# Depthwise convolution and SwiGLU on one core: own input tiles for the first pair of each sequence, group 0's ScalarE products one chunk later, joins one chunk later, two swaps moved behind the marks

## The chip, the core and the metric

One NeuronCore of a Trainium2 chip runs the kernel. TensorE (PE) multiplies, VectorE (DVE), ScalarE (ACT) and GpSimd (POOL) work on tiles, SyncE (SP) issues most transfers. Each engine works through an instruction list of its own, in order. The metric is device time in microseconds of one execution; lower is better.

## What is computed

The reference, cut to what matters:

```python
# x: (8, 4096, 192) float32, weight: (8 heads, 7 taps)
w = softmax(weight, axis=-1)                       # 7 taps per head of 24 channels
x_pad = concatenate([zeros((B, 6, D)), x], axis=1) # each sequence starts from zeros
y[b, s, c] = sum_k w[head(c), k] * x_pad[b, s + k, c]
# y as (32768, 192); w_gate, w_val: (192, 1536); w_out: (1536, 192)
g = y @ w_gate
out = (g * sigmoid(g) * (y @ w_val)) @ w_out       # float32
```

A causal convolution with seven taps runs over each of the 8 sequences separately, and a gated feed-forward block over all 32768 tokens.

## The kernel before

**Tiling.** The tokens are cut into 64 blocks of 512, and two blocks make a pair `q` (1024 tokens, 32 pairs, four to a sequence: `ppb = 4`). The 1536 hidden columns are 12 chunks of 128 (`NCH`). A chunk of a block is the unit of the schedule: `first(j)` writes the gate and the value of chunk j with six matmuls (L397, L398; two at a time, one on each half of PE's rows), `gate(j)` takes silu on ACT (L402) and the product `h` on DVE (L404), and `second` does four output units (L409) that use the `h` of the block before. The gate has two PSUM buffers, so the gate matmuls of chunk j+2 wait for the silu of chunk j; the value has three.

**Convolution of the next pairs.** It runs beside these matmuls, on DVE, ACT and POOL, one to two pairs ahead. A pair has three groups: group 0 is channels 0 to 127 of its first block, group 2 the same channels of its second block, group 1 channels 128 to 191 of both blocks, on the two halves of the partitions. For each group, `plan_group` places these steps on chunks:

- `emit_load` (SP): four parts of x into the tiles `sqA` and `sqB`, as squares of 32 tokens by 32 channels, with 32 tokens of history (`HIST`) ahead.
- `emit_turn` (DVE, L100): transposes the squares into `xtA` or `xtB`.
- `emit_blank` (ACT, L104): only for `q % ppb == 0`, the first pair of a sequence: overwrites the history in `xtA` and `xtB` with zeros. There are seven such pairs (q = 4, 8, ..., 28); pair 0 has its own opening code.
- `start_d` (ACT, L334) and `dve_tap` (DVE, L344): a running sum of taps in `run`, at the end in `aD`.
- `act_tap` (ACT, L327): two products t; `pool_tap` (POOL, L349 and the add L356): two or three products, added up.
- `join` (POOL): adds ACT's two products (L356) and then `aD` (L362), which gives the convolved tile `xc`.
- `swap` (SP, L310 and L311): two transfers that copy `xc` into `xs` with its partition halves exchanged, which the matmuls need beside `xc`.

**Order.** `at_chunk(c, f)` hangs a step on chunk c. After a chunk's own instructions (matmuls, copy `o` L447 and store L439 where a half of a block is done, silu, product) the steps of that chunk follow in the order in which they were registered. A pair q is used from chunk 24q on. Its group 0 starts at 24q-28, group 1 at 24q-20, group 2 at 24q-12, and the offsets in `PLAN` count from there: the turn at -2, ACT's products at +2 and +4, DVE's taps at +1 and +3 (group 1 only +1), POOL's taps and the join at +4, the swap at +11. The second pair, `q == 2`, has its own swap offsets (`swap2`), pair 1 a table of its own (`opening`). The loads stand at 24q-47, -40, -34 and -28.

**Marks.** Two output units of opposite halves share a PSUM bank. Where the second half follows, PE must not begin before the first is done: `mark` (L304) puts an empty instruction into SP's list that waits for PE's last unit of the first half, and PE's next unit waits for this mark. Marks stand at chunks 1, 7, 13 and 19 of every 24, two at a time, ahead of the steps of the same chunk, and PE waits for them in the chunk that follows. SP's list holds marks, loads, swaps and stores in one order, so a swap that waits for its `xc` holds back every mark behind it.

**A pair in numbers of chunks, modulo 24.** Swaps before: group 0 at 7, group 1 at 15, group 2 at 23. ACT's copies `o`: at 4, 10, 16 and 22. ACT's steps for group 0: 20 (start), 22 and 0; group 1: 4, 6, 8; group 2: 12, 14, 16.

Of the kernel before, what the change touches and what calls it, by code (L numbers as in the profile page):

```python
# [11 lines left out]

PLAN = dict(
    start=(-28, -20, -12), turn=-2,
    acts=(2, 4), dves=(1, 3), pool=4, swap=11, swap2=(18, 16, 14), npool=(2, 3, 2),
    load=(-47, -40, -34, -28),
    opening=(
        (3, 5, (8,), (7, 9), 4, 10, 15),
        (9, 11, (12, 14), (13,), 11, 15, 21),
        (14, 16, (18, 20), (17, 18), 20, 20, 28),  # L20
    ),
# [5 lines left out]
def kernel(  # L27
# [9 lines left out]
    nc = tc.nc  # L37
    fp32 = mybir.dt.float32
# [5 lines left out]
    B, S, D = x.shape  # L44
# [3 lines left out]
    P = 128  # L48
    DB = D - P
    grp = D // H  # L50
    SUBS = 4
    TB = P * SUBS
    NCH = Dff // P
# [4 lines left out]
    n_pairs = NT // (2 * TB)  # L58
    ppb = S // (2 * TB)
    x_flat = x.flatten_outer_dims()  # L60

    const_pool = ctx.enter_context(tc.tile_pool(name="const", bufs=1))
    wpool = ctx.enter_context(tc.tile_pool(name="wts", bufs=1))
    xpool = ctx.enter_context(tc.tile_pool(name="xin", bufs=2))
# [8 lines left out]
    SQ = 32  # L73
    HIST = SQ
    squares, xts = {}, {}

    def emit_load(q, part):
        if part == 0:
            squares[q, "A"] = xpool.tile([P, HIST + 2 * TB], fp32, tag="sqA", name="sqA")
            squares[q, "B"] = xpool.tile([P, HIST + TB], fp32, tag="sqB", name="sqB")  # L80
        for k in range(2):
            quad = 2 * (part % 2) + k
            if part < 2:
                tile_, t0, n, c = squares[q, "A"], 0, 2 * TB, SQ * quad
            else:
                tile_, t0, n, c = squares[q, "B"], TB * (part % 2), TB, P + SQ * k
            row = q * 2 * TB + t0 - HIST
            n = n // SQ + 1
            nc.sync.dma_start(  # L89
                out=tile_[quad * SQ : (quad + 1) * SQ, :].rearrange("p (n c) -> p n c", c=SQ),  # L90
                in_=x_flat[row : row + n * SQ, c : c + SQ].rearrange("(n p) c -> p n c", p=SQ),
            )

    def emit_turn(q, g):
        name, lo, hi = (("A", 0, HIST + TB), ("B", 0, HIST + TB), ("A", HIST + TB, HIST + 2 * TB))[g]
        if g < 2:
            xts[q, name] = xpool.tile(
                list(squares[q, name].shape), fp32, tag=f"xt{name}", name=f"xt{name}"
            )
        nc.vector.transpose(out=xts[q, name][:, lo:hi], in_=squares[q, name][:, lo:hi])  # L100

    def emit_blank(q, g):
        rows = slice(0, (P, DB)[g])
        nc.scalar.copy(xts[q, "AB"[g]][rows, 0:HIST], zeros[rows, 0:HIST])  # L104

    def sync_after(ins, earlier, why="one bank, two halves of the array"):
        tc.add_manual_dep(
# [8 lines left out]
    for lo, hi in ((0, 2), (2, SUBS), (SUBS, 2 * SUBS)):  # L116
        nc.sync.dma_start(  # L117
            out=x_sb[:, lo:hi, :],
            in_=x_flat[lo * P : hi * P, :].rearrange("(s p) d -> p s d", p=P),
        )  # L120
    if n_pairs > 1:
        for part in range(4):
            emit_load(1, part)
# [10 lines left out]
    def load_w(lo, hi, which):  # L134
# [3 lines left out]
    zeros = const_pool.tile([P, TB], fp16, tag="zeros", name="zeros")  # L138
# [10 lines left out]
        out=mask, in_=mask, pattern=[[1, D]],  # L149
# [3 lines left out]
        out=mask, in_=mask, pattern=[[-1, D]],  # L153
# [315 lines left out]
    for k in range(1, 5):  # L469
        v, s = tapA1(k)  # L470
        nc.vector.scalar_tensor_tensor(
            out=sumA1, in0=v, scalar=s, in1=sumA1, op0=ALU.mult, op1=ALU.add
# [18 lines left out]
    def at_chunk(c, f):  # L491
        todo.setdefault(c, []).append(f)

    def plan_group(q, g, turn, start, acts, dves, pool, join, swap):
        made = []
        at_chunk(turn, lambda: emit_turn(q, g))
        if g < 2 and q % ppb == 0:
            at_chunk(start, lambda: emit_blank(q, g))

        def step(c, f):  # L500
            def run():
                if not made:
                    made.append(Group(q, g))
                f(made[0])

            at_chunk(c, run)

        ks = iter(range(1, K))
        step(start, lambda group: group.start_d())
        for k, c in zip(ks, acts):  # L510
            step(c, lambda group, k=k: group.act_tap(k))
        ks = list(range(1 + len(acts), K))
        for k, c in zip(ks, dves):
            step(c, lambda group, k=k: group.dve_tap(k, k == len(acts) + len(dves)))
        for k in ks[len(dves) :]:
            step(pool, lambda group, k=k: group.pool_tap(k))
        step(join, lambda group: group.join())
        step(swap, lambda group: group.swap())


    def lateC(step):
# [8 lines left out]
        else:  # L530
            nc.scalar.copy(D2b, late["sum"][:, 0, :])

    late = {}
    for step, c in enumerate((0, 1, 3, 5)):
        at_chunk(c, lambda step=step: lateC(step))

    if n_pairs > 1:
        for g, plan in enumerate(PLAN["opening"]):
            plan_group(1, g, *plan)
    for q in range(2, n_pairs):  # L540
        base = 2 * NCH * q
        for part, c in enumerate(PLAN["load"]):
            at_chunk(base + c, lambda q=q, part=part: emit_load(q, part))
        for g in range(3):
            c = base + PLAN["start"][g]
            plan_group(
                q, g, c + PLAN["turn"], c, [c + o for o in PLAN["acts"]],
                [c + o for o in PLAN["dves"][: 4 - PLAN["npool"][g]]],
                c + PLAN["pool"], c + PLAN["pool"],
                c + (PLAN["swap2"][g] if q == 2 else PLAN["swap"]),  # L550
            )


# [85 lines left out]
```

## Time and profile before

| | |
|---|---|
| median of 3 runs | 777.34 us (777.27 to 777.89) |
| profiled execution | 777.53 us, its span 775.8 us |
| PE busy | 768.8 us, 99% of the span |
| POOL busy | 669.2 us, 86% |
| DVE, ACT busy | 659.5 us, 659.4 us, 85% each |
| TensorE clock granted | 1.00 |
| 16 DMA engines, mean | 87 GB/s |

Busy time of PE is modelled and matmuls overlap, so 99% doesn't say that PE loses nothing: whether it does is seen from the starts of matmuls that should follow each other at a fixed distance. Times in the views are microseconds from the start of the span, and a line of the timeline gives start, duration, engine, line, operation and tiles, with the idle time ahead of it in brackets.

### The profile page before, as it was taken

What the parts mean: (1) busy time and instruction counts of PE and PEld (TensorE: products, weight loads), DVE (VectorE), ACT (ScalarE), POOL (GpSimd) and SP (SyncE); (2) the same over time, 40 slices, a digit from 0 to 9 for tenths busy, and PEclk for the clock granted to TensorE, in tenths of its full rate; (3) what the DMA queues carried; (4) which work ended last, traced back from release to release, by engine and by line L of the source; (5) the groups of instructions that cost most, each with busy time, mean ns of one, the idle gap of its engine ahead of it and who ended that gap; (6) DMA issues with size and microseconds to landing.
All of it is one profiled execution on the core that took longest, in us unless ns stands there. A gap on an engine that the chain in (4) does not pass through costs nothing.

```text
span 775.8 us, 27812 instructions
## 1 busy us (share of the span) xinstructions
PE 768.8 (99%) x10824; PEld 527.3 (68%) x10824; DVE 659.5 (85%) x1040; ACT 659.4 (85%) x1206; POOL 669.2 (86%) x642
## 2 busy tenths in 40 slices
PE   9999999999999999999999999999999999999998
PEld 3666667666666666666666666667666666766666
DVE  6988888888888888888888888888888888888875
ACT  6888888888888888888888888888888888888874
POOL 5999999988989989889898889998899988999920
PEclk9999999999999999999999999999999999999999
DMA  9434343443344444343443434443443443434211
GB/s 178 81 82 95 76 96 82 89 98 82 77 93 91 82 91 90 80 91 81 96 83 86 92 82 88 97 83 78 92 90 83 93 90 77 91 84 94 56 43 53
DMA packets 255828, 67.24 MB, mean 87 GB/s; under 512 B 209104, under 2 KB 255312, under 8 KB 255696
## 3 DMA queue, kind: packets, MB, share of 16 engines
q1 hardware_dynamic: 253296, 63.70, 38.9%
q0 software_dynamic: 2384, 1.77, 1.5%
q8 instruction: 84, 1.38, 0.8%
q14 instruction: 48, 0.39, 0.2%
q10 hardware_dynamic: 16, 0.00, 0.0%
HBM read 29.72 MB, written 25.17 MB: 71 GB/s over the span
## 4 chain that ended last, share of the span: by engine, by line
PE 94%; SPq 3%; ACT 2%; DMA 0%; DVE 0%; issue 0%
PE gate L397 55%; PE acc L409 32%; PE val L398 7%; SPq L89 2%; ACT silu L402 1%; ACT run L334 1%; DMA sqA<-in_x_dram 0%; SPq L311 0%; SPq L117 0%; DVE h L404 0%; PE val L409 0%; PE run L409 0%; ACT xtB L104 0%; SPq L310 0%; DVE xtA L100 0%
## 5 line engine op out<-in xcount | busy, mean ns | idle before, releaser
L404 DVE TENSOR_TENSOR h<-silu,val 128x512 f16<-128x512 f16 x768 | 506.8, 680 | 105.6 <-ACT silu L402 72.0
L402 ACT ACTIVATE silu<-gate 128x512 f16<-128x512 f32 x768 | 449.8, 594 | 101.0 <-PE val L398 85.3
L356 POOL TENSOR_TENSOR t<-t,t 128x512 f32<-128x512 f32 x310 | 393.7, 1270 | 46.2 <-ACT t L327 21.1
L398 PE MATMUL val<-xc,w_sb 64*128 64x512 f16 x1116 | 409.9, 376 | 0.0
L397 PE MATMUL gate<-xc,w_sb 64*128 64x512 f16 x1116 | 409.5, 376 | 0.4
L409 PEld LDWEIGHTS <-h 64*128 64x128 f16 x6144 | 296.6, 94 | 126.8 <-SPq L304 1.7
L409 PE MATMUL acc<-wo_sb,h 64*128 64x192 f16 x6096 | 368.6, 243 | 0.5 <-SPq L304 0.3
L397 PE MATMUL gate<-xs,w_sb 64*128 64x512 f16 x1128 | 364.5, 376 | 0.0
L398 PE MATMUL val<-xs,w_sb 64*128 64x512 f16 x1128 | 364.4, 376 | 0.0
L397 PEld LDWEIGHTS <-w_sb 64*128 64x128 f16 x2304 | 209.5, 94 | 103.2 <-issue 2.1
L398 PEld LDWEIGHTS <-w_sb 64*128 64x128 f16 x2304 | 204.0, 94 | 6.3 <-issue 4.0
L362 POOL TENSOR_TENSOR xc<-t,aD 128x512 f16<-128x512 f32 x93 | 118.3, 1272 | 7.7 <-DVE aD L344 0.4
L349 POOL TENSOR_SCALAR t<-xtA,wn 128x512 f32<-128x512 f32 x125 | 85.3, 696 | 5.8 <-DVE xtA L100 3.4
L327 ACT ACTIVATE t<-xtA,wn 128x512 f32<-128x512 f32 x123 | 88.1, 716 | 0.0
L349 POOL TENSOR_SCALAR t<-xtB,wn 128x512 f32<-128x512 f32 x93 | 63.8, 695 | 7.9 <-ACT xtB L104 6.4
L447 ACT COPY o<-acc 128x384 f32<-128x384 f32 x126 | 60.3, 479 | 3.2
L344 DVE SCALAR_TENSOR_TENSOR run<-xtA,wn,run 128x512 f32<-128x512 f32 x62 | 46.4, 749 | 0.0
L344 DVE SCALAR_TENSOR_TENSOR aD<-xtA,wn,run 128x512 f32<-128x512 f32 x62 | 46.0, 741 | 0.0
L100 DVE STREAM_TRANSPOSE xtA<-sqA 128x544 f32<-128x544 f32 (+1 forms) x62 | 44.7, 721 | 0.6 <-DMA sqA<-in_x_dram 0.6
L327 ACT ACTIVATE t<-xtB,wn 128x512 f32<-128x512 f32 x62 | 44.3, 714 | 0.0
L334 ACT ACTIVATE run<-xtA,wn 128x512 f32<-128x512 f32 x62 | 42.6, 687 | 0.4 <-DVE xtA L100 0.2
L344 DVE SCALAR_TENSOR_TENSOR aD<-xtB,wn,run 128x512 f32<-128x512 f32 x31 | 23.0, 741 | 0.0
(88 smaller groups left out, 142.4 us busy)
## 6 DMA issues: line engine op xcount, KB each, us to landing
out_dram<-o SPq DMA_DIRECT2D x128, 192.0 KB, 2.2
sqA<-in_x_dram SPq DMA_DIRECT2D x124, 132.0 KB, 3.2
xs<-xc SPq DMA_DIRECT2D x186, 64.0 KB, 2.0
sqB<-in_x_dram SPq DMA_DIRECT2D x124, 68.0 KB, 2.3
wo_sb<-in_moe_w_out_dram POOLq DMA_DIRECT2D x1, 576.0 KB, 10.1
x_sb<-in_x_dram SPq DMA_DIRECT2D x2, 192.0 KB, 2.5
x_sb<-in_x_dram SPq DMA_DIRECT2D x1, 384.0 KB, 4.6
w_sb<-in_moe_w_gate_dram POOLq DMA_DIRECT2D x1, 384.0 KB, 7.0
```

Source lines behind the costliest of these rows:

```text
L327: mul(parts[-1], *self.tap(k))
L334: nc.scalar.mul(self.aD, *self.tap(0))
L344: nc.vector.scalar_tensor_tensor(out=self.aD, in0=v, scalar=s, in1=run, op0=ALU.mult, op1=ALU.add)
L349: self.product(k, lambda t, v, s: nc.gpsimd.tensor_scalar(t, v, scalar1=s, scalar2=1.0, op0=ALU.mult, op1=ALU.mult), self.parts)
L356: nc.gpsimd.tensor_tensor(self.parts[0], self.parts[0], t, op=ALU.add)
L362: nc.gpsimd.tensor_tensor(xc, self.parts[0], self.aD, op=ALU.add)
L397: nc.tensor.matmul(g, w[0:DB, ca, f], a[0:DB, :], start=(i == 0), stop=(i == 2))
L398: nc.tensor.matmul(v, w[DB:P, cb, f], b[DB:P, :], start=(i == 0), stop=(i == 2))
L402: nc.scalar.activation(s, self.g.pop(j), AF.Silu)
L404: nc.vector.tensor_tensor(h, s, self.v.pop(j), op=ALU.mult)
L409: ins = nc.tensor.matmul(acc, self.h[j][r, ts(s, P)], wo_r[r, j, :], start=first and j == 0, stop=not first and j == NCH - 1, skip_group_c ...
L447: nc.scalar.copy(self.o[:, 2 * half : 2 * half + 2, :], self.acc[:, :, 0:D])
```

## The change

The offsets of the plan become one entry for each group, the first pair of a sequence gets tiles of its own, and POOL clears their history once:

```diff
-    acts=(2, 4), dves=(1, 3), pool=4, swap=11, swap2=(18, 16, 14), npool=(2, 3, 2),
+    acts=((3, 5), (2, 4), (2, 4)), dves=(1, 3), pool=4, join=5, npool=(2, 3, 2),
+    swap=(11, 15, 13), swap2=(18, 16, 14),
...
+    headA = const_pool.tile([P, HIST + 2 * TB], fp32, tag="headA", name="headA")
+    headB = const_pool.tile([P, HIST + TB], fp32, tag="headB", name="headB")
+
     def emit_load(q, part):
+        head = q % ppb == 0
         if part == 0:
-            squares[q, "A"] = xpool.tile([P, HIST + 2 * TB], fp32, tag="sqA", name="sqA")
-            squares[q, "B"] = xpool.tile([P, HIST + TB], fp32, tag="sqB", name="sqB")
+            squares[q, "A"] = headA if head else xpool.tile(
+                [P, HIST + 2 * TB], fp32, tag="sqA", name="sqA"
+            )
+            squares[q, "B"] = headB if head else xpool.tile(
+                [P, HIST + TB], fp32, tag="sqB", name="sqB"
+            )
...
-            row = q * 2 * TB + t0 - HIST
-            n = n // SQ + 1
+            skip = HIST if head and t0 == 0 else 0
+            row = q * 2 * TB + t0 - HIST + skip
+            n = n // SQ + 1 - skip // SQ
             nc.sync.dma_start(
-                out=tile_[quad * SQ : (quad + 1) * SQ, :].rearrange("p (n c) -> p n c", c=SQ),
+                out=tile_[quad * SQ : (quad + 1) * SQ, skip:].rearrange("p (n c) -> p n c", c=SQ),
...
-    def emit_blank(q, g):
-        rows = slice(0, (P, DB)[g])
-        nc.scalar.copy(xts[q, "AB"[g]][rows, 0:HIST], zeros[rows, 0:HIST])
...
-        if g < 2 and q % ppb == 0:
-            at_chunk(start, lambda: emit_blank(q, g))
...
+    def blank():
+        nc.gpsimd.memset(headA[:, 0:HIST], 0.0)
+        nc.gpsimd.memset(headB[0:DB, 0:HIST], 0.0)
+
+    if n_pairs > ppb:
+        at_chunk(2 * NCH, blank)
...
-                q, g, c + PLAN["turn"], c, [c + o for o in PLAN["acts"]],
+                q, g, c + PLAN["turn"], c, [c + o for o in PLAN["acts"][g]],
...
-                c + PLAN["pool"], c + PLAN["pool"],
-                c + (PLAN["swap2"][g] if q == 2 else PLAN["swap"]),
+                c + PLAN["pool"], c + PLAN["join"],
+                c + PLAN["swap2" if q == 2 else "swap"][g],
```

Modulo 24, ACT's products of group 0 stand at chunks 23 and 1 in place of 22 and 0; the swap of group 0 stays at 7, that of group 1 goes from 15 to 19, that of group 2 from 23 to 1 of the pair's own first block. The lists of PE and DVE keep their order. On POOL the two memsets are new, at chunk 24; the joins keep their place among POOL's instructions. On ACT the 14 blanks fall away and group 0's two products each stand behind one more silu. On SP the swap of group 1 now follows the marks of chunk 19 and stands ahead of a load, and the swap of group 2 follows the marks of chunk 1.

## The prediction

> **What bounds the kernel now.** I read the page's busy times and chain first, then PE's timeline for the distance between chunks, then the engine that ended each odd distance, then the waits.
>
> ```profile
> PE 768.8 (99%) x10824; PEld 527.3 (68%) x10824; DVE 659.5 (85%) x1040; ACT 659.4 (85%) x1206; POOL 669.2 (86%) x642
> PE 94%; SPq 3%; ACT 2%; DMA 0%; DVE 0%; issue 0%
> ```
>
> PE carries the chain, so only what makes PE wait can be won. The timeline gives the starts of each chunk's first gate matmul: 0.978 us apart, with 1.308 and 0.648 where a half block ends, and 11.730 us for a block in which nothing waits. Block by block from block 4 on (61.3 us) to block 62, the excess over 11.730 sums to 3.29 us, in 31 places. Ahead of them the change moves only pair 2's products, where PE loses 0.015 us; behind them, nothing. Three kinds make up the sum.
>
> The first, at the end of chunk 0 of a pair; PE's and ACT's timeline of one of them:
>
> ```profile
> 132.75 0.38 PE L397 MATMUL gate<-xc,w_sb 64*128 64x512 f16 x1
> ...
> 133.77 0.37 PE L397 MATMUL gate<-xc,w_sb 64*128 64x512 f16 x1
> ```
>
> ```profile
> 131.34 0.48 ACT L447 COPY o<-acc 128x384 f32<-128x384 f32 x1
> 132.03 0.60 ACT L402 ACTIVATE silu<-gate 128x512 f16<-128x512 f32 x1 [0.20 <-PE val L398]
> 132.52 0.71 ACT L327 ACTIVATE t<-xtA,wn 128x512 f32<-128x512 f32 x1
> 133.13 1.07 ACT L402 ACTIVATE silu<-gate 128x512 f16<-128x512 f32 x2
> ```
>
> 132.75 to 133.77 is 1.02 where 0.978 is the rule: the gate of chunk 1 waits for the silu of chunk 23, which stands behind copy, silu and product of chunk 22. It recurs at 22 pairs, 0.0435 us each.
>
> The second, at the seven first pairs of sequences, group 1; ACT's timeline, then three pieces of the chain:
>
> ```profile
> 184.84 0.60 ACT L402 ACTIVATE silu<-gate 128x512 f16<-128x512 f32 x1
> 185.33 0.20 ACT L104 CAST xtB<-zeros 64x32 f32<-64x32 f16 x1
> 185.57 0.69 ACT L334 ACTIVATE run<-xtB,wn 128x512 f32<-128x512 f32 x1
> 186.20 1.06 ACT L402 ACTIVATE silu<-gate 128x512 f16<-128x512 f32 x2
> ```
>
> ```profile
> 185.57 0.69 ACT run L334
> 186.26 0.52 ACT silu L402
> 186.83 0.37 PE gate L397
> ```
>
> The blank pushes start and silu back, and PE's gate of chunk 7 begins 0.227 us late; without a blank, other pairs show no delay here.
>
> The third, marks behind swaps, in SP's and PE's timeline:
>
> ```profile
> 80.12 0.47 SPq L310 DMA_DIRECT2D xs<-xc  x1
> 80.63 0.60 SPq L311 DMA_DIRECT2D xs<-xc  x1
> 81.33 0.53 SPq L439 DMA_DIRECT2D out_dram<-o  x1
> ```
>
> ```profile
> 82.05 0.50 PE L409 MATMUL acc<-wo_sb,h 64*128 64x192 f16 x8 [0.33 <-SPq L304]
> ```
>
> POOL comes late out of the opening, so pair 3's swaps of groups 1 and 2 wait for `xc`, the first until 80.12 as shown, the second until 86.86, with the marks behind them. PE loses 0.519 us at 82.05 and 0.233 at 88.15. Both are single events.
>
> **The change, part by part.** *Blanks.* 14 casts of 0.20 us leave ACT. Only those of group 1 end a wait of PE: 7 x 0.227 = 1.59 us. The chain behind them then is that of other pairs, where the silu ended at 116.07 and PE's gate started at 116.13: 0.06 us of room, with 0.04 from silu's end to PE's start at 186.83. What is late next is nothing, but barely.
>
> *Group 0's products.* Chunk 22 keeps the copy, so silu 23 starts when PE's value ends, at 132.61 in the frame above; the product follows 0.48 later (as at 110.11 to 110.59), silu 0 another 0.61 later, at 133.71, ready since 133.58. It ends at 134.31, and PE asks for it at 134.70. The product at chunk 1 puts silu 2 at 135.64, 0.7 us ahead of need. So 22 x 0.0435 = 0.95 us go and nothing replaces them.
> POOL adds the second product at +2.21 us from the pair's start (629.45, pair start 627.24, waiting 0.32). It now exists at about +3.05, so POOL is up to 0.85 later there, and `xc` of group 0 is done at +5.7 in place of +4.8; its swap stands behind marks at +8.2. Group 1's follows at about +14.5, group 2's at +21.3; they were +13.7 and +20.8. The new places of their swaps come at +20 and +26. No wait on this path reaches PE.
>
> *Joins at 5.* The join keeps its place among POOL's instructions: 0.
>
> *Memsets.* Not in the trace at this size; the memsets of 128x1 took 0.10, of 128x128 0.19, of 8x192 0.25. Two cost 0.2 to 0.5 us of POOL at 42.3 us; by the 128x128 row I take 0.4. POOL then is busy back to back until about 95 us, so every later `xc` of pairs 2 and 3 moves by 0.4. Pair 2's swap of group 1 left at 58.39 and landed 2.3 later; PE asks at 61.75, so 1.1 us cover it. Cost 0.
>
> *Swaps on SP.* Behind the marks of chunk 67, pair 3's group 1 finds `xc` done (80.12 + 0.4, the marks at about 81.1), and the marks wait for no swap: 0.52 + 0.23 = 0.75 us go. What queues behind the moved swaps (1.1 us of issue): a load, needed by its turn 5 us later, and a store that waited for ACT anyway. Group 2's swap at chunk 25 is needed at chunk 36.
> Group 1's is the tight one. Its second half, L311, left 8 us ahead of the first value matmul that reads it; now it leaves about 3.00 us before the pair's start, by the distance from marks to L311 at group 0's swap (93.87 to 94.52), and the value asks at +0.45: 3.40 us to land. The tile's view gives the landings:
>
> ```profile
> DMA to landing us min/median/max: 1.9/2.0/4.0
> ```
>
> 4 of the 85 recorded L311 took over 3.40. The trace's transfer records tie the slow ones to PE's instruction fetches, 16 KB packets every 9 us at fixed places of PE's list: a fetch 1.0 to 1.3 us after L311 went with landings of 3.14, 3.30, 3.32, 3.45, 3.69 and 3.82. In 7 of the 29 pairs a fetch stands 1.75 to 2.2 us before the pair's start, so 0.8 to 1.25 after the new L311. Bounds: 0, and 7 x (4.00 - 3.40) = 4.2 us. The mean of those six landings over 3.40 is 0.12, so 0.8 us; but the two longest had fetches of 1.5 and 1.6 us, and these seven took 0.9 to 1.1. I take half, 0.4 us.
> The Trainium skill speaks to this twice. "Runtime: NRT & Kernel Launch", section "Instruction fetch mechanics", says that crossing a 16 KiB block costs one queue bump, mostly hidden: by that nothing is lost and the time is 774.05. "DMA: Bandwidth & Descriptors", section "Issuing engines are not separate DMA queues", says that all transfers interleave on the same 16 engines whoever issued them: by that a fetch can delay a swap, and the trace's 3.1 to 4.0 us agree.
>
> *Loads.* One square of 33 or 17 fewer: 0. Seven pairs' silus take over the second wait that other pairs' have: 0, as those show no delay.
>
> **Sum.** Gain 1.59 + 0.95 + 0.75 = 3.29, return 0.4. The profiled execution took 777.53 (span 775.8, 1.7 around it), 0.19 over the median of the runs; against the median, 777.34 - 3.29 + 0.4 = 774.45. I forecast 774.4. Measurement can tell about 0.2%, 1.55 us: below 775.8 is faster, above 778.9 slower.
>
> **Rivals.**
> *The swap lands late in most pairs* (the other side). Place: the first value matmul of a pair. The time equals before at 0.11 us a pair over 29 pairs, and is slower by 0.2% from 0.17, when landings average 3.57. At the bound of 0.6 in every pair, 774.05 + 17.4 = 791.5; with the seven fetches alone at 0.6, 778.3. Against: 56 of 85 landed within 2.3 us. Chance 0.09, of it 0.04 slower.
> *The wait at the pair's start stays or moves.* ACT's work is the same; room at chunk 7 is 0.02 us. Then 0.95 is not won: 775.4. For: the same sum of copy, silu and product within three chunks. Against: the instants above, 0.4 us clear. Chance 0.10.
> *The marks still wait.* POOL's lateness is in time, not in chunks, and PE runs 0.75 us ahead; group 0's swap of pair 4 meets `xc` at 93.57 + 0.4 just behind marks at about 93.1. If a later mark catches it, 0.75 stays: 775.2. Against: the next marks are 5.9 us on. Chance 0.05.
> *POOL becomes the bound.*
>
> ```profile
> POOL t L356 <- ACT t L327: 21.1, 48, 0.6
> ```
>
> POOL's 16 instructions of a pair sum to 21.4 us, 22.4 with 0.08 ahead of each of 13; a pair is 23.5. Were the 0.85 added to waits that use up the 1.1 of room, each pair would grow by 0.85: 799. Against: the product is late by the same in each pair, so POOL shifts once. Chance 0.02.
> *It does not do what it says*: a wait not seen takes the gain, 777.3. Chance 0.04.
>
> **Numbers.** The forecast holds 0.70, from 773.8 to 775.1. Faster: 0.70 + 0.10 + 0.05 + 0.02 of the late landing = 0.87. Slower: 0.04 + 0.02 = 0.06. Same: 0.07. The range 773.6 to 776.0 takes in the stalls that might stay, 775.2 and 775.4, and landings up to 2 us in all; 0.13 is left out.
>
> **What would show it.** Right: blocks of 11.730 us at even and odd places; no L104; no chunk 0 of 1.02; SP's swap of pair 3 after the marks and no PE wait on L304; POOL's wait on L327 moved to group 0's second product, about 1 us. Wrong: PE's value matmul waiting for `xs` at a pair's start, the seven pairs with a fetch first; gates waiting for silu at chunk 7 of every pair; POOL's `xc` later from pair to pair.

## The result, and the profile after

The changed kernel takes 774.17 us (median of 6 runs, 773.64 to 774.68), the kernel before beside it 777.30 us (6 runs, 776.81 to 777.89). The ratio is 0.9960, with a 95% interval of 0.9947 to 0.9973: 3.1 us faster. The forecast was 774.4 us.

The profiled execution took 774.68 us, its span is 773.0 us. That is 2.8 us less than before's span, although the steady part won more: from the start of block 4 to the start of block 63, before needs 695.36 us (61.30 to 756.67) and after 692.09 us (61.73 to 753.82), 3.27 us less. The rest is the opening, in which the first chunk of this execution began at 13.17 us and in before's at 12.73 us. In the fourteen profiles of this study the first chunk begins at 12.0 to 13.3 us, in no order that follows the edits. For that reason I compare the runs below by the stretch from block 4 to block 63, and by its *excess*: what blocks 4 to 62 took over 11.730 us each. Before it was 3.29 us; after it is 0.022 us, nearly all of it in block 27.

The page's lines for the engines and for the chain, after:

```profile
PE 766.7 (99%) x10824; PEld 614.8 (80%) x10824; DVE 661.3 (86%) x1040; ACT 662.7 (86%) x1192; POOL 668.5 (86%) x644
PE 96%; SPq 3%; DMA 0%; DVE 0%; issue 0%; DVEq 0%
```

ACT is gone from the chain, where it had 2%. PE's share of weight loads went from 68% to 80% with as many loads as before; that looks like more work and is none, as the last section shows. Now the three places of the prediction, one by one. First the pair's start, ACT's and PE's timeline after (start, duration, engine, line, operation, tiles; idle time ahead in brackets). This is pair 5, whose first chunk starts at 132.11:

```profile
130.70 0.48 ACT L454 COPY o<-acc 128x384 f32<-128x384 f32 x1
...
131.98 0.60 ACT L409 ACTIVATE silu<-gate 128x512 f16<-128x512 f32 x1
132.47 0.71 ACT L334 ACTIVATE t<-xtA,wn 128x512 f32<-128x512 f32 x1
133.08 0.59 ACT L409 ACTIVATE silu<-gate 128x512 f16<-128x512 f32 x1
133.93 0.60 ACT L409 ACTIVATE silu<-gate 128x512 f16<-128x512 f32 x1 [0.26 <-PE val L405]
134.42 0.71 ACT L334 ACTIVATE t<-xtA,wn 128x512 f32<-128x512 f32 x1
```

```profile
132.11 0.38 PE L404 MATMUL gate<-xc,w_sb 64*128 64x512 f16 x1
...
133.09 0.38 PE L404 MATMUL gate<-xc,w_sb 64*128 64x512 f16 x1
```

The product now stands behind silu 23, and chunk 1 follows chunk 0 after 0.98 us in place of 1.02. Second, the first pair of a sequence, ACT's timeline after:

```profile
184.11 0.60 ACT L409 ACTIVATE silu<-gate 128x512 f16<-128x512 f32 x1
184.61 0.69 ACT L341 ACTIVATE run<-xtB,wn 128x512 f32<-128x512 f32 x1
185.22 1.18 ACT L409 ACTIVATE silu<-gate 128x512 f16<-128x512 f32 x2
```

No cast stands between silu and start; the start is issued 0.50 us behind the silu, where before it came 0.73 us behind it. Third, SP's timeline at pair 3's swap of group 1, after:

```profile
81.66 0.47 SPq L317 DMA_DIRECT2D xs<-xc  x1
82.18 0.59 SPq L318 DMA_DIRECT2D xs<-xc  x1
```

The marks of chunk 19 are ahead of it in SP's list, and no swap holds up a mark any more. Two weight loads still wait for a mark, 0.25 us each, in blocks 27 and 57; the 0.023 us of block 27 are lost there, as the last section shows. What came in exchange is the tight swap. SP's and PE's timeline after, at the start of pair 8:

```profile
199.48 0.59 SPq L318 DMA_DIRECT2D xs<-xc  x1
```

```profile
202.71 0.38 PE L404 MATMUL gate<-xs,w_sb 64*128 64x512 f16 x1
202.73 0.38 PE L405 MATMUL val<-xs,w_sb 64*128 64x512 f16 x1
202.92 0.38 PE L404 MATMUL gate<-xc,w_sb 64*128 64x512 f16 x1
203.01 0.37 PE L405 MATMUL val<-xs,w_sb 64*128 64x512 f16 x1
```

This transfer landed 3.49 us after its issue, by the transfer records; the median of the tile is 2.0 us. The value matmul that reads it begins 0.09 us behind its gate matmul, where 0.02 is the rule. It is the only late one in this execution, and the gates go on at their distance: PE lost nothing here. Pairs 5, 8, 13, 16, 21, 24 and 29, those that the prediction counted, with an instruction fetch 1.75 to 2.2 us ahead of the pair's start in before, are those with long landings at the new place (2.9 to 3.5 us in one of the two transfers); the others landed in 1.9 to 2.3 us where recorded.

### The profile page after: what moved, and what is told of

Read it like the earlier page. It is cut to its first block, busy times and chain, and to the rows that moved or that the text cites. A ratio compares the mean times of both kernels' runs of the same rounds, so it can differ in the third digit from the quotient of the medians.

```text
span 773.0 us, 27821 instructions
## 1 busy us (share of the span) xinstructions
PE 766.7 (99%) x10824; PEld 614.8 (80%) x10824; DVE 661.3 (86%) x1040; ACT 662.7 (86%) x1192; POOL 668.5 (86%) x644
## 4 chain that ended last, share of the span: by engine, by line
PE 96%; SPq 3%; DMA 0%; DVE 0%; issue 0%; DVEq 0%
PE gate L404 44%; PE acc L416 31%; PE val L405 20%; SPq L100 2%; DMA sqA<-in_x_dram 0%; PE val L416 0%; SPq L124 0%; DVE h L411 0%; SPq L318 0%; DVE xtA L111 0%; SPq L317 0%; DVE aD L351 0%; DVE xtB L111 0%; DVE o L621 0%; PE run L416 0%
## 5 line engine op out<-in xcount | busy, mean ns | idle before, releaser
L416 PEld LDWEIGHTS <-h 64*128 64x128 f16 x6144 | 345.7, 94 | 77.0 <-SPq L311 0.8
L416 PE MATMUL acc<-wo_sb,h 64*128 64x192 f16 x6096 | 393.3, 243 | 0.0
L111 DVE STREAM_TRANSPOSE xtA<-sqA 128x544 f32<-128x544 f32 (+1 forms) x48 | 34.6, 721 | 0.2 <-DMA sqA<-in_x_dram 0.2
```

The lines of the kernel that those rows point to most:

```text
L416: ins = nc.tensor.matmul(acc, self.h[j][r, ts(s, P)], wo_r[r, j, :], start=first and j == 0, stop=not first and j == NCH - 1, skip_group_c ...
```

## The experiments

Each starts from the changed kernel. A short table first; "steady" is block 4 to block 63 in the profiled execution. Each ratio is to runs of the kernel before that were taken beside it, whose medians lie between 777.30 and 777.84 us, so medians taken beside different runs of before are comparable to about 0.5 us.

| run | median us (runs) | ratio to before, 95% | steady us | excess us |
|---|---|---|---|---|
| before | 777.30 (6) | | 695.36 | 3.29 |
| after | 774.17 (6) | 0.9960 (0.9947–0.9973) | 692.09 | 0.02 |
| blanks back | 775.87 (10) | 0.9976 (0.9967–0.9985) | 693.74 | 1.67 |
| products early | 775.31 (6) | 0.9970 (0.9957–0.9982) | 693.32 | 1.25 |
| swaps early | 775.22 (6) | 0.9969 (0.9957–0.9981) | 692.91 | 0.84 |
| copy, not read | 774.96 (5) | 0.9969 (0.9956–0.9982) | 692.97 | 0.90 |
| swap two chunks later | 777.81 (10) | 1.0007 (0.9998–1.0016) | 695.97 | 3.90 |
| halves exchanged | 774.19 (4) | 0.9957 (0.9944–0.9971) | 692.08 | 0.01 |
| halves exchanged, again | 773.99 (5) | 0.9954 (0.9941–0.9968) | 692.08 | 0.01 |
| after, again | 774.79 (5) | 0.9962 (0.9949–0.9974) | 692.28 | 0.21 |
| fetches moved | 775.75 (1) | | 693.14 | 1.07 |
| opening, turn and tap later | 775.29 (9) | 0.9973 (0.9963–0.9983) | 692.08 | 0.01 |
| opening, start later | 774.66 (5) | 0.9961 (0.9947–0.9975) | 693.34 | 1.27 |
| the same, halves exchanged | 774.71 (5) | 0.9957 (0.9945–0.9970) | 692.07 | 0.00 |

**Each of the three gains taken back alone.** First the blanks: the first pairs use ordinary tiles again, and ACT writes the zeros.

```diff
-        head = q % ppb == 0
+        head = False
...
+    def emit_blank(q, g):
+        rows = slice(0, (P, DB)[g])
+        nc.scalar.copy(xts[q, "AB"[g]][rows, 0:HIST], zeros[rows, 0:HIST])
...
+        if g < 2 and q % ppb == 0:
+            at_chunk(start, lambda: emit_blank(q, g))
```

> The changed kernel with the blanks on ScalarE back (and the first pairs in the ordinary tiles), products, joins and swaps as changed. Theory, that the blank of group 1 holds up start and silu: PE's gate of chunk 7 is 0.227 us late at seven pairs again, 1.6 us in all, about 775.8 us. Rival, that these waits came from ScalarE's work being late at chunks 22 to 1 and the products' new place alone cures them: no excess over 11.730 us a block, 774.2 us.

Blocks 6, 14, 22, 30, 38, 46 and 54 took 0.226 to 0.228 us more each, 1.59 us together. The other 0.08 us is in block 48, a late landing (below). ACT's timeline of this run, where the start again comes 0.23 us behind the issue of a cast of 0.20 us:

```profile
184.15 0.60 ACT L413 ACTIVATE silu<-gate 128x512 f16<-128x512 f32 x1
184.65 0.20 ACT L115 CAST xtB<-zeros 64x32 f32<-64x32 f16 x1
184.88 0.69 ACT L345 ACTIVATE run<-xtB,wn 128x512 f32<-128x512 f32 x1
185.51 1.07 ACT L413 ACTIVATE silu<-gate 128x512 f16<-128x512 f32 x2
```

Second, group 0's products:

```diff
-    acts=((3, 5), (2, 4), (2, 4)),
+    acts=((2, 4), (2, 4), (2, 4)),
```

> The changed kernel with group 0's products back at 2 and 4. Theory, that the product behind chunk 22 delays silu 23: chunk 0 of a pair takes 1.02 us again in place of 0.978, 0.0435 us a pair, and at the first pairs of sequences too, since their silus now have the second wait of the others: 29 pairs, 1.26 us, about 775.4 us. Rival, that the swaps' new places cured it: no excess, 774.2 us.

Every even block from 2 to 60 took 0.042 to 0.045 us more, 29 of them from block 4 on, 1.25 us together. In before it was 22: the seven blocks in which the blank of group 1 cost 0.227 us are among them now. So the parts overlap by 7 x 0.0435 = 0.30 us, and the three runs' losses, 1.59 + 1.25 + 0.84 = 3.68 us, are more than the 3.29 us won together.

Third, the swaps:

```diff
-    swap=(11, 15, 13),
+    swap=(11, 11, 11),
```

> The changed kernel with all swaps at 11, as before. Theory, that marks behind pair 3's swaps cost 0.52 and 0.23 us once each: both are back, 0.75 us or a little more since POOL runs 0.4 us later, about 774.9 us, and all other blocks stay at 11.730 us; the value matmul of pair 8 no longer begins late. Rival, that PE, once freed of the other waits, runs ahead and more swaps hold up marks: excess in more pairs than the third.

Block 5 took 0.601 us more and block 6 took 0.235, nothing else. SP's and PE's timeline of this run show the place of before again, the swap at 80.38 and PE's unit that waits for the mark behind it:

```profile
80.89 0.60 SPq L318 DMA_DIRECT2D xs<-xc  x1
```

```profile
82.31 0.51 PE L416 MATMUL acc<-wo_sb,h 64*128 64x192 f16 x8 [0.41 <-SPq L311]
```

The first event is a little larger than in before (0.60 in place of 0.52 us). Counted from the start of block 2, `xc` of that swap was done 0.02 us later than in before and PE came to block 5 0.06 us earlier, since it no longer waits in the first blocks of pairs 1 and 2. No value matmul was late in any pair of this run, though landings of over 3 us occur in it too: with the swap four chunks earlier they come in time.

**What in a blank costs 0.227 us?** A copy of the same size at the same place, but into a spare tile that nothing reads:

```diff
+    spare = const_pool.tile([DB, HIST], fp32, tag="spare", name="spare")
...
+        if g == 1 and q % ppb == 0:
+            at_chunk(start, lambda: nc.scalar.copy(spare, zeros[0:DB, 0:HIST]))
```

> The changed kernel with one copy of 64x32 zeros to a spare tile on ScalarE ahead of group 1's start at the seven first pairs: the time of the blank without its wait for the turn and with nobody waiting for its result. Theory, that ScalarE's time alone counts: the gate of chunk 7 is late by 0.2 us at seven pairs, 1.4 to 1.6 us, about 775.7 us. Rival, that the blank cost by waiting for VectorE's turn or by keeping POOL waiting: no excess, 774.2 us.

The seven blocks took 0.092 to 0.102 us more, not 0.227: neither the 0.2 us of the theory nor the nothing of the rival. ACT's timeline of this run:

```profile
183.38 0.60 ACT L410 ACTIVATE silu<-gate 128x512 f16<-128x512 f32 x1
183.87 0.20 ACT L506 CAST spare<-zeros 64x32 f32<-64x32 f16 x1
183.98 0.69 ACT L342 ACTIVATE run<-xtB,wn 128x512 f32<-128x512 f32 x1
184.60 1.06 ACT L410 ACTIVATE silu<-gate 128x512 f16<-128x512 f32 x2
```

The start is issued 0.11 us behind the cast, with the cast's 0.20 us still running; when it reads what the cast writes, it comes 0.23 us behind. So 0.09 of the 0.227 us is the copy's own place in ACT's list, and 0.13 us is the start waiting for the copy's result. A further 0.225 us in block 29 is a single silu issued 0.29 us late; what held it isn't shown.

**The tight swap.** How near is the edge? Group 1's swap two chunks later, at chunk 21:

```diff
-    swap=(11, 15, 13),
+    swap=(11, 17, 13),
```

> The changed kernel with group 1's swap two chunks later, behind the load of chunk 20: the half that the pair's first value matmul reads leaves about 1.85 us ahead of the pair in place of 3.0. Theory, that only landings delayed by PE's instruction fetches are late: ordinary ones (2.0 us) are in time at +0.15 for +0.45; the seven pairs with a fetch 1.75 to 2.2 us ahead land at about +1.0 to +1.4 and PE loses 0.4 to 0.8 us each, the two with a fetch 0.1 to 0.4 us ahead land at about +2 and lose 1.5: 5 to 9 us in nine pairs, 779 to 783 us. Rival, that landings are as slow as the mean of all pairs would need: some loss in every pair. Rival, that PE absorbs a late half: 774 to 775 us.

This takes back all that the change won (ratio 1.0007, 0.9998 to 1.0016): 3.9 us of excess, less than I had expected. Ten blocks have it: the first blocks of six of the seven pairs with a fetch (all but pair 29), those of pairs 11 and 23, and blocks 27 and 57. Pair 23 lost 0.33 us: its landing took 2.90 us with no 16 KB fetch within 3 us of its issue, and what made it long isn't shown. The direction held; the size didn't, since only part of a late value is lost. The dearest event, SP's and PE's timeline of this run at the start of pair 21:

```profile
506.62 1.92 SPq L317 DMA_DIRECT2D xs<-xc  x1
508.58 0.60 SPq L318 DMA_DIRECT2D xs<-xc  x1
```

```profile
510.64 0.37 PE L405 MATMUL val<-xs,w_sb 64*128 64x512 f16 x1 [0.72 <-DMA xs<-xc]
510.99 0.38 PE L404 MATMUL gate<-xc,w_sb 64*128 64x512 f16 x1
511.19 0.38 PE L405 MATMUL val<-xc,w_sb 64*128 64x512 f16 x1
```

The issue of L317, otherwise 0.47 us, took 1.92 us with a fetch at the same time, and L318 stood behind it. The value matmul at 510.64 is 1.10 us behind its gate matmul; the next chunk's is 0.20 us behind, and block 42 lost 0.90 us. So it is in every such event of this study: 0.743 of distance cost 0.544, 1.014 cost 0.814, 0.914 cost 0.715. What is over 0.196 us is lost there, within 0.005 us, and what is under it isn't.

Do the fetches make the landings long? Thirty small matmuls in PE's opening shift the fetches against the blocks by about 2.1 us:

```diff
+    for _ in range(30):
+        nc.tensor.matmul(early["idle"][:, 0:8], zeros[:, 0:P], zeros[:, 0:8], start=True, stop=True)
```

> The changed kernel with 30 matmuls of 8 columns more at PE's start, 60 instructions, which moves every later instruction fetch of PE about 2.1 us earlier against its work. Theory, that fetches make landings late: the landings over 2.8 us of group 1's second half are no longer those of pairs 5, 8, 13, 16, 21, 24 and 29 but of pairs 3, 11, 19 and 27, whose fetches stood 0 to 0.4 us ahead of the pair's start. Rival, that stores or loads of the same pairs do it: the same pairs as before. The time may be up to 2 us longer in the opening.

The long landings of the swap's second half (2.97 us or more) and of its first half (3.23 us or more) went to pairs 3, 6, 11, 14, 19, 22, 27 and 30, which now have a fetch 1.4 to 2.4 us ahead of their start; pairs 5, 8, 13, 16, 21, 24 and 29 are back at 1.9 to 2.83 us where recorded. I had not foreseen that 6, 14, 22 and 30 would be among the late ones. All fourteen traces say the same of the swaps of every group: from 60 us on, 634 recorded transfers had such a fetch beginning between 0.5 us before their issue and 1.75 us after it, and 383 of them took over 2.8 us to land; of the 1508 others 9 did. 0.52 us of the excess of this run is a mark that stood behind a store whose issue took 1.74 us; SP's and PE's timeline of this run:

```profile
74.53 1.74 SPq L448 DMA_DIRECT2D out_dram<-o  x1
```

```profile
76.46 0.51 PE L418 MATMUL acc<-wo_sb,h 64*128 64x192 f16 x8 [0.15 <-SPq L313]
```

**Taking the late landing away.** The third value matmul of a pair's first chunk is the first to read group 1's `xs`, the half that the second transfer writes; the other half is first read a block later. The two transfers of group 1 in the other order:

```diff
+        if tag == "xs1":
+            nc.sync.dma_start(out=sw[DB:P, :], in_=xc[0:DB, :])
         nc.sync.dma_start(out=sw[0:DB, :], in_=xc[DB:P, :])
-        nc.sync.dma_start(out=sw[DB:P, :], in_=xc[0:DB, :])
+        if tag != "xs1":
+            nc.sync.dma_start(out=sw[DB:P, :], in_=xc[0:DB, :])
```

> The changed kernel with group 1's two transfers in the other order, so that the half which is read first leaves 0.5 us earlier. Theory, that the one value matmul of pair 8 that began 0.07 us late waited for this landing: no value matmul is late, value and gate matmuls keep one distance of 0.02 us from end to end, PE's weight loads go back from 80 to about 68% of the span, the time stays at 774.2 us within 0.1. Rival, that the distance has another origin: it appears again.

No value matmul was late, the distance of value to gate stayed at 0.025 us to block 57, and the excess was 0.012 us. The transfer that now leaves second took 3.65 us in pair 8 and cost nothing. The page's line for this kernel has PE's weight loads at 69%, with the same x10824:

```profile
PE 765.8 (99%) x10824; PEld 530.3 (69%) x10824; DVE 661.2 (86%) x1040; ACT 660.6 (86%) x1192; POOL 667.9 (87%) x644
```

**The opening.** Two attempts to win in blocks 0 and 1, and neither did. The turn of the opening's group 1 a chunk later, and a tap of its group 2:

```diff
-        (9, 11, (12, 14), (13,), 11, 15, 21),
-        (14, 16, (18, 20), (17, 18), 20, 20, 28),
+        (10, 11, (12, 14), (13,), 11, 15, 21),
+        (14, 16, (18, 20), (17, 19), 20, 20, 28),
```

> The changed kernel with two steps of pair 1 moved on VectorE: group 1's turn from chunk 9 to 10, group 2's last tap from 18 to 19, so that no tap and turn follow each other without a product between. Theory, that such couples hold up the product and with it PE's value matmul (0.69 and 0.43 us in the opening): up to 1.1 us less, 773.1 to 773.6 us. Rival, that ScalarE's start of group 1 or POOL's sum then comes late and holds the first pairs: 774.2 us or more.

775.29 us (9 runs; ratio 0.9973, 0.9963 to 0.9983): slower than the changed kernel by about 1.1 us. Block 1 took 14.21 us in place of 13.04. Of these 1.17 us, 0.49 are in chunk 13, where ACT's start waits for the turn, as this run's ACT timeline shows; another 0.57 are in chunk 22, and what caused those isn't shown:

```profile
26.37 0.69 ACT L341 ACTIVATE run<-xtB,wn 128x512 f32<-128x512 f32 x1 [1.18 <-DVE xtB L111]
```

Then the whole of that group, start, products, taps and join, one chunk later:

```diff
-        (9, 11, (12, 14), (13,), 11, 15, 21),
+        (10, 12, (13, 15), (14,), 12, 15, 21),
```

> The changed kernel with pair 1's group 1 one chunk later as a whole (turn at 10, start at 12, products at 13 and 15, tap at 14), group 2 as it was. Theory, that the moved turn of e7_opening cost by making ScalarE's start wait 1.18 us for it with two silus behind: with the start moved too, chunk 13 takes no longer than the 1.68 us of the changed kernel and chunk 22 stays at 1.19, so the time is 773.5 to 774.3 us. Rival, that VectorE's turn itself is what comes late whatever stands behind it: chunk 13 at 2 us or more, 774.6 us or more.

774.66 us (774.18 to 776.30). Block 1 took 13.12 us in place of 13.04: chunk 13 shrank by 0.08 us to 1.60, as the theory asked, but three others grew by 0.04 to 0.08, chunk 22 among them (1.27 us), so the forecast time was missed. But the profiled execution, at 776.30 us the slowest of the five, showed something else: 1.27 us of excess, of it 0.133 + 0.269 + 0.181 + 0.349 + 0.086 = 1.02 in the first blocks of pairs 5, 8, 16, 24 and 29, and 0.25 in blocks 27 and 57. The five are late landings (3.75 to 3.82 us in pairs 8, 16 and 24), with the swap at the same place as in the changed kernel. Was this the edit, or does the changed kernel do so in some executions? Three kernels, run beside one another, asked that.

**Again, on one chip.** The changed kernel once more, with no edit:

> The changed kernel once more, nothing edited. Theory (the swap's late landing is a matter of the single execution): the excess of blocks 4 to 62 over 11.730 us lies anywhere from 0 to 1.3 us, all of it at first blocks of pairs 5, 8, 13, 16, 21, 24 and 29, and each loss is the value's new lateness less what it was before, once that is over 0.196 us; median 774.0 to 774.8. Rival (the losses of the run with the opening's start moved, 1.05 us in blocks 10, 16, 32, 48 and 58, came from that edit): at most 0.05 us of excess, as in the first profile of the changed kernel, and a median of 774.2.

The kernel with the halves exchanged once more:

> The two transfers of group 1's swap in the other order, once more, beside the changed kernel on the same chip. Theory: the half that the first value matmul reads leaves 0.52 us sooner, so no landing up to 3.9 us is late; excess at most 0.05 us whatever the execution, and a median below that of the changed kernel of this call by what the late landings cost on average, 0.1 to 0.6 us. Rival: the order is worth nothing, the medians agree within 0.1 us.

And the last opening together with the exchanged halves:

> The opening's start of group 1 moved by one chunk, as in the run that lost 1.05 us at late values, and the two transfers in the other order as well. Theory: the losses in blocks 10, 16, 32, 48 and 58 go, and the excess falls from 1.27 to 0.2 us or less; median 774.1 to 774.6. Rival (the losses come from the opening's edit and not from this landing): they stay, 1 us or more.

The changed kernel took 774.79 us (774.45 to 775.08), with 0.206 us of excess: 0.087 at the start of pair 24, whose landing took 3.68 us (3.20 in the first profile), and 0.121 in block 57. So a late landing costs the unedited kernel time in some executions, as the theory said; that all of the loss would be in first blocks missed. PE's timeline of this run at pair 24's start, where the value that reads `xs` is 0.28 us behind its gate and the next gate comes 0.63 us after that, with 0.55 as the rule:

```profile
578.11 0.38 PE L404 MATMUL gate<-xc,w_sb 64*128 64x512 f16 x1
578.39 0.37 PE L405 MATMUL val<-xs,w_sb 64*128 64x512 f16 x1
...
578.74 0.38 PE L404 MATMUL gate<-xc,w_sb 64*128 64x512 f16 x1
...
578.93 0.38 PE L405 MATMUL val<-xc,w_sb 64*128 64x512 f16 x1
```

With the halves exchanged the time was 773.99 us (773.81 to 774.76) and 0.005 us of excess; with the opening's edit as well 774.71 us (773.62 to 774.83), with no excess at all and a block 1 of 13.13 us. The opening's edit by itself doesn't make landings long: in this last run those recorded of the seven pairs took 3.10 to 3.32 us. For the same reason this run doesn't show what the exchange saves, since a landing of 3.49 us cost the changed kernel nothing either. That the landings caused the losses is seen in the run that had them, where each late value whose landing is recorded began 0.04 us after it. Both time forecasts missed: 0.80 us below the changed kernel in place of 0.1 to 0.6, and 774.71 us in place of 774.1 to 774.6.

How much the exchanged halves win in the median is not settled: 0.0 us between medians of two separate comparisons, 0.8 side by side, and the ratios' intervals overlap. The steady stretch says 0.01 to 0.2 us for the two profiles of the changed kernel. This version has the lowest ratios to before, 0.9957 and 0.9954 against 0.9960 and 0.9962 of the changed kernel, but isn't measurably faster.

## Why the prediction was right, step by step

**What bounds the kernel** held: only what made PE wait was won, and from block 4 to block 63 PE lost 3.29 us before and 0.02 us after.

**Blanks, 7 x 0.227 = 1.59 us.** Right: taking them back alone cost 1.59 us in the seven blocks named. What the prediction had left open was why a cast of 0.20 us costs 0.227: 0.09 is its own time and 0.13 the wait of the start for its result. "Nothing late next, but barely" held as well: blocks 6, 14, ... take 11.730 us.

**Group 0's products, 22 x 0.0435 = 0.95 us.** Right, and so are the instants. From the pair's start, silu 23 was put at -0.14, the product at +0.34, silu 0 at +0.96, silu 2 at +2.89; the trace has -0.13, +0.36, +0.97 and +2.93. The rival that the wait stays or moves (775.4 us) fell by this.

**POOL.** The second product was put at +3.05 us from the pair's start, `xc` at +5.7. In pair 26, whose first chunk starts at 624.79, POOL adds the product at 627.96, +3.17, and `xc` is done at 630.58, +5.79. POOL's waits for a product cost PE nothing, and in sum they didn't grow. Before, the view has 48 of 0.44 us for ACT and 15 of 0.32 us under the name of a transfer, which stand at the same places and end the same 0.14 us after a product of ACT; with 8.8 us of waits for blanks that makes 34.7 us. After, it is 50 of 0.69 us, at group 0's two products of each pair, 34.5 us. The prediction had about 1 us at the second product; there it was 0.68 us, as POOL now waits as long at the first. The waits' view after, in total, times and longest:

```profile
POOL t L363 <- ACT t L334: 18.1, 26, 0.7
POOL t L363 <- DVE h L411: 16.4, 24, 0.7
```

The lateness didn't add up from pair to pair, so the rival in which POOL becomes the bound fell.

**Memsets, 0.4 us of POOL, cost 0.** They took 0.12 and 0.11 us, and the next instruction began 0.16 us after the first of them. The price was too high by the choice of its row, the memset of 128x128: counted from the start of block 2, pair 3's `xc` of group 1 was done 0.05 us later than in before, and not 0.4. The cover held.

**Marks, 0.75 us.** Right: 0.84 us when taken back alone, in the two blocks named. The rival that a later mark catches a swap fell: no PE wait in the trace after has that cause.

**The swap's second half, 0.4 us returned.** This is the term that was mis-sized, and its place was right. The pairs, 5, 8, 13, 16, 21, 24 and 29, are those in which it is long; moving the fetches moved it; exchanging the halves took it away. But the changed kernel lost about 0.0 and 0.2 us to it in its two profiles, 0.08 us with the blanks back and 1.27 us in the run with the moved opening. The price rested on six landings, whose mean over 3.40 us is 0.13 and not 0.12; two more recorded ones with a fetch at the same distance, 3.06 and 3.20 us, were left out, and with them the mean is 0.10. Two further reasons: the prediction priced each landing over 3.40 us in full, while a value that is up to 0.196 us late costs no gate at that place; and a landing beside a fetch is not a constant, the same transfer of pair 24 with the fetch at nearly the same distance (1.80 to 1.93 us ahead of the pair's start) took 3.20, 3.68 and 3.82 us. What these executions lost, 0.0 to 1.27 us, lies between the prediction's ends of 0 and 4.2.

**Sum.** 3.29 won and 0.02 returned in the steady stretch make 3.27 us; the runs' medians give 3.13 and, in the second comparison, 3.01 us. The prediction's 2.9 is within 0.4 us of all three, less than the 1.3 us by which the start of the first chunk varies from profile to profile, so the agreement of the medians to 0.2 us is in part luck.

## What to carry to other kernels

When a bound engine's work comes at a fixed distance, list every distance that differs, name what ended it, and price a change by those rows alone: three small kinds of wait made up the whole difference here, while the shares of busy time barely moved. When a transfer is moved nearer to its reader, compare its longest landings, and not the median, with the time that is left, and see which half the reader asks for first: sending that half first gave 0.52 us of room for nothing. And read a gain of a few tenths of a per cent block by block, since the start of the first chunk varied by 1.3 us from profile to profile, more than two of the three parts, though the code ahead of it is the same in all of them but one.

## What was not expected

**The gate's and the value's matmuls slip against each other.** They run on the two halves of PE's rows, usually 0.02 us apart. A late operand of the value lets its matmuls fall behind by up to 0.196 us while the gates go on; the lag then stays for dozens of blocks. In the second run of the changed kernel it stayed at 0.196 us from block 48 to chunk 9 of block 57, where it fell to 0.075 and the gate lost the same 0.121 us. Block 27 is another such place (in the first profile 0.090 to 0.068 us, at 0.023 us of loss). At both places a mark comes late. Two marks stand side by side in SP's list, and SP reaches the second 0.08 to 0.11 us after the first everywhere else from block 4 on; in these two blocks it took 0.38 to 0.40 us, in this run and in ten others. PE's weight load waits for it, here in block 57 of the second run:

```profile
691.90 0.35 PEld L416 LDWEIGHTS <-h 64*128 64x128 f16 x8 [0.25 <-SPq L311]
```

With values and gates 0.025 us apart the same wait cost at most 0.014 us, so it is the lag that makes it dear. What holds SP there isn't shown.

**The share of weight loads follows that lag and not the work.** The profile's share counts the time in which at least one load runs. By that, 10824 loads of 94 ns took 68% of the span before, 80% after, 64% with the swaps early and 69% with the halves exchanged, though after and the last of these have the same steady time, 692.09 and 692.08 us. The loads of the two halves overlap more or less: over the blocks of all fourteen traces in which the lag stays the same, the share is 0.64 at a lag of 0.00 us, 0.70 at 0.02, 0.90 at 0.09, 0.94 at 0.12 and 0.78 at 0.196. "Perfetto Trace Analysis" in the Trainium skill, section "Identifying the Most-Contended Engine", recommends, beside another measure, the summed time of the weight loads over the window to judge how near TensorE is to its limit. The profile's share isn't that sum: summed, the loads take 1.31 of the span before and 1.32 after, and the sum doesn't follow the lag. With two streams of loads it is over 1 here, while the profile's share moved by 11 points with nothing gained or lost; neither followed the time here.

**Instruction fetches lengthen other transfers.** A fetch of 16 KB beside a swap took its landing from 2.0 us to as much as 4.0 us, and an issue on SP from 0.47 to 1.92 us or from 0.4 to 1.74 us. "Runtime: NRT & Kernel Launch" in the Trainium skill, section "Instruction fetch mechanics", calls the cost of such a crossing mostly hidden. For the engine that fetches, no run here shows otherwise; the transfers beside it paid.

**A small operation on ACT cost PE more than twice as much when the next one read its result**, 0.227 us against 0.09, for casts of the same size at the same place.
